# A product of layer one's mixing taken as seven smaller products, with its sums made on chip

## The chip, the cores and the metric

The kernel runs on one core of a Trainium2 chip. The metric is the device time of one execution in microseconds (us), the median of several runs. The engines are called as in the profile: PE is the matrix engine (TensorE), DVE the vector engine, ACT the scalar engine, POOL GpSimd, and SP the engine whose queue issues nearly all the DMAs here.

## The reference

Two layers, each an attention block without softmax and a gated mixer, both added to x (2048 rows of 512):

```python
def _A_ref(x, wqkv, wo):        # 32 heads of 16
    q, k, v = split(x @ wqkv)
    phi = lambda t: where(t > 0, t + 1, exp(t)) + 1e-6
    kv = einsum("bhsd,bhse->bhde", phi(k), v)
    z  = einsum("bhsd->bhd", phi(k))
    o  = einsum("bhqd,bhde->bhqe", phi(q), kv) / (einsum("bhqd,bhd->bhq", phi(q), z) + 1e-6)
    return o @ wo

def _B_ref(x, w_in, w_sp, b_sp, w_out):
    z = gelu(x @ w_in)                       # 512 -> 1792
    z1, z2 = z[..., :896], layernorm(z[..., 896:])
    g = einsum("ts,bsf->btf", w_sp, z2) + b_sp      # w_sp is 2048 x 2048
    return (z1 * g) @ w_out

x = A_x
for _ in range(2):
    x = x + _A_ref(layernorm(x), A_wqkv, A_wo)
    x = x + _B_ref(layernorm(x), B_w_in, B_w_sp, B_b_sp, B_w_out)
```

The change is about the sum over `w_sp`, the mixing.

## The kernel before, in words

**Precision.** Each float32 operand is split into a high part (by ACT) and a low part, the rest (by DVE's `low`, L173, sometimes by POOL, L178). A product is then three matmuls, high by high, high by low and low by high (L184 to L186 for most stages, L1520 to L1522 in the mixing's products).

**Stages of a layer.** The first stage, `P1`, walks over 16 tiles of 128 rows in a loop `s` = 1 to 17: it normalises, makes keys and queries (K, Q; phi at L471, L474, L486; the sum of keys at L492 on POOL) and accumulates the sums G in four banks. `transition` takes G out (L670), sums the keys (zb), multiplies G by the weights of v, masks the blocks (L696) and multiplies by the weights of the output (L706). The second stage, `P2`, is a loop `s` = 1 to 18: it finishes attention (den at L755 to L757, division at L764, product `c`), adds x (`c2`, L798), takes statistics (L315, L317 on DVE; L319 to L322 on POOL), normalises (L328 on ACT), and makes z2 and, in `f`, z1. The transposes and the splits of the next tiles stand between. The third stage, `P4`, is the mixing and the product with `w_out` (`out7`).

**The mixing.** `w_sp` and z2 are seen as 2 x 2 blocks, and the block product is made with seven products instead of eight; their order is `ORDER = ("P2", "P1", "P6", "P7", "P4", "P5", "P3")`. Four of these (P6, P7, P5, P3) multiply sums of blocks of `w_sp`. `Sums` makes these sums in layer one and stores them in DRAM (`s1` to `s4`, float32) for both layers: a `tick` stores the two sums of the last tick, loads up to three pages of `w_sp` ahead, and makes two sums with POOL (L1260). There are 32 ticks for 64 sums of 256 KB. In layer one, eight ticks are in `P1` (steps 2 to 9, in tiles borrowed from the big buffers), fourteen in `P2` (steps 5 to 18) and ten in the first ten steps of the mixing, that is in P2 and in the first steps of P1 (of the mixing).

**Divided products.** A product named in `DIVIDED[layer]` is itself made by the same scheme, as seven smaller ones. An ordinary product has 8 steps `k` of 24 matmuls (8 column groups of 128x512 by three); a divided one has 14 steps of 12 (4 groups by three), two steps for each of the seven, in the order `SEVEN = (1, 5, 6, 2, 7, 3, 4)`. After each pair `evac_div` takes the banks out and combines them. The sums of z2's quarters are made by `zsum` and `zpart` on chip; four sums of quarters of `w_sp`, the tensors `hP` in DRAM (8 pieces of 512 KB for each product), are made before by `halve`: a copy from DRAM to DRAM (SP's queue), then a DMA that adds to what is there (POOL's queue, L1250), each tied `behind` the split of a step's weights. `PARTS` says at which step which of the 32 DMAs goes out. In before only P4 is divided in layer one, and P2 and P4 in layer two; P4's `hP` is made while P1, P6 and P7 of layer one run, P2's while P4 and P5 of layer one run, for layer two.

**What sets the order.** Nothing is scheduled by a program: each engine runs its instructions as the code writes them. Buffers are taken and given back by hand: 22 pages (128x512, `pg`), 6 quads (`qd`), 4 big ones (`bg`, seven sheets of 128x512 each) and 8 PSUM banks. The queue of SP is in order: a store that waits for its data holds up the loads behind it. In the mixing, `fetch(g)` asks for the weights of step g, `sp(g)` splits them (L1350 on ACT, L1351 on DVE), `mm(g)` issues the matmuls, `evac` takes the banks out. `LEAD` says how many steps ahead `P1` loads, `ln_a`, `ln_b` and turns its tiles.

Of the kernel before, what the change touches and what calls it, by code (L numbers as in the profile page):

```python
# [13 lines left out]
OP = mybir.AluOpType  # L14
# [55 lines left out]
        self.slots.put(*self.tiles)  # L70


DIVIDED = (("P4",), ("P2", "P4"))


WRAW = {("P5", 3): (0, 3), ("P5", 6): (1, 4), ("P3", 1): (2, 5), ("P3", 4): (6,)}
# [2 lines left out]
WLONE = ("P3", 5)  # L79
WZ = (0, 1, 2, 3, 4, 5, 6, 7, 8, 9, 10, 11, 12, 13, 14, 15)  # L80
FIRST = 6
LEAD = 6
FIRSTPAIR = 4
EXTRA = (2, 3, 4, 5, 16, 17)
WSTORE = 9
FS = {6: 1, 12: 1, 17: 1}
PARTS = {("P1", k): k - 2 for k in range(2, 8)} | {("P6", k): 6 + k for k in range(8)}
PARTS |= {("P7", 0): 14, ("P7", 1): 15} | {("P4", 2 * k): 16 + k for k in range(7)}
PARTS |= {("P4", 13): 23} | {("P5", k): 24 + k for k in range(8)}


class Sheets:
# [18 lines left out]
def mixer_kernel(ctx: ExitStack, tc: tile.TileContext, x_in, wqkv, wo_d, win1_d, win2_d, wsp_d, bsp_d, wout_d,  # L111
# [291 lines left out]
    class P1:  # L403
# [185 lines left out]
        def run(self, sums):  # L589
            side = deque([self.win2] * NF)  # L590
            ND = NT - DEFER
            for s in range(1, NT + 2):
                for i in self.ahead(s, LEAD - 1, 3):
                    self.loadx(i)
                for i in self.ahead(s, LEAD + 1, 1):
                    self.turn.load(i)
                if 2 <= s < NT:
                    self.T_high(s)
                if s == 1:
                    if not self.kb:  # L600
# [12 lines left out]
                if s == NT + 1:  # L613
                    self.late()
                if s <= NT:
                    self.xsplit(s - 1)
                    self.K_split(s - 1)
                for i in self.ahead(s, LEAD, 2):
                    self.ln_b(i)
                if s <= ND:  # L620
                    self.Q_phi(s - 1)
                if s >= 2:
                    self.Gmm(s - 2)
                if s == NT + 1:
                    self.late_phi()
                if self.L == 0:
                    if s == 2:
                        sums.slots = Sheets(bigs, 2)
                    if 2 <= s < 10:
                        sums.tick(s < 9)  # L630
                    if s == 10:
                        sums.store()
                        sums.slots.close()
                        sums.slots = pages
                if s == 11:
                    self.wv = quads.get([P, 4, 512])
                    nc.sync.dma_start(self.wv, wqkv[:, 1024:1536].rearrange("(c p) f -> p c f", p=P))
                if s == 14:
                    self.wo = quads.get([P, 4, 512])
                    nc.sync.dma_start(self.wo, wo_d.rearrange("(c p) f -> p c f", p=P))  # L640
                if s in range(3,NT-1):
                    self.turn.pre(s + 1)
                if self.L:
                    if s <= 4:
                        self.win2.load(2)
                    else:
                        self.win2.piece()
                    if s == NT - 1:
                        self.win2.sums()
                    if s == NT:  # L650
                        self.win2.last()
                    continue
                if s > 3 and side:
                    side.popleft().piece()
                if s > 2 and side:
                    side[0].fetch()


    def transition(p1, p2):
# [5 lines left out]
        pages.put(za)  # L665
        p1.late()
        p1.wk.free()
        g = quads.get([P, 4, 512])
        for c in range(4):
            (high if c % 2 == 0 else nc.vector.tensor_copy)(g[:, c, :], p1.G[c])  # L670
            banks.put(p1.G[c])
        zb = banks.get(PAGE)
        nc.tensor.matmul(zb, ones, zh, start=True, stop=False)
        nc.tensor.matmul(zb, ones, zl, start=False, stop=True)
# [47 lines left out]
    class P2:  # L722
# [300 lines left out]
        def run(self, sums):  # L1023
# [2 lines left out]
                return  # L1026
            w1 = self.win1
            for s in range(1, NT + 3):
                self.loadx(s + 1)
                self.qturn.load(s + 1)  # L1030
                if s in self.qturn.by_pe:
                    self.c(s - 1)
                    self.b_high(s)
                    self.c2(s - 1)
                    self.p1.late_phi_b()
                    self.b_low(s)
                    if s >= 2:
                        self.d_high(s - 2)
                        self.d_low(s - 2)
                    self.p1.late()  # L1040
                    self.c3(s - 1)
                    self.a2(s + 2)
                    self.p1.late_phi_a()
                    self.a(s + 3)
                else:
                    if s < NT:
                        self.b_high(s)
                    self.a2_den(s + 2)
                    if s < NT:
# [30 lines left out]
                w1.fetch()  # L1080
                if self.L == 0:
                    if s > 4:
                        sums.tick()
# [129 lines left out]
    class Sums:  # L1213
# [3 lines left out]
        def __init__(self):  # L1217
# [2 lines left out]
            self.ahead = deque(self.todo)  # L1220
            self.raw, self.made, self.done = {}, [], []
            self.slots = pages
            self.parts, self.halves = [], {}
# [4 lines left out]
            self.parts = [(what, p, m, q) for p in ("P4", "P2") for what in ("copy", "add") for m in (1, 3, 2, 4)  # L1228
                          for q in range(2)]

        def fetch(self):
# [5 lines left out]
        def halve(self, n, after):  # L1237
# [7 lines left out]
            if what == "copy":  # L1245
                nc.sync.dma_start(self.halves[p, m, q], src)
            else:
                if m in (2, 4):
                    src = self.halves[p, m // 2, q]
                behind(nc.gpsimd.dma_start(self.halves[p, m, q], src, accum_op=OP.add, max_dma_last_dim=4096), after)  # L1250

        def store(self):

# [30 lines left out]
    class P4:  # L1284
# [559 lines left out]
        def run(self, nxt):  # L1844
# [9 lines left out]
            while p2.f():  # L1854
                self.zahead(min(self.zmade, 3))
                n += 1
                if early and n == 4:
                    self.sp(1)
                    self.fetch(5)
            self.zahead(3)  # L1860
            if p2.win1 is not None:
                p2.win1.free()
            if not early:
                self.sp(1)
                self.fetch(5)
            self.gb = [bigs.get([P, NF, 512]) for _ in range(NCHK)]
            n = len(self.steps)
            for g in range(n):
                p, k = self.steps[g]
                self.fetch(g + 5)  # L1870
                evac_first = (p == "P6" or p == "P1" and nxt is not None) and k == HT - 1
                div_first = p in self.div and k == 13 and p == "P4"
                if not evac_first and not div_first:
                    self.sp(g + 2)
                    self.zahead(g + 4 if p in ("P2", "P1") else g + 4)
                self.mm(g)
                if evac_first:
                    if p == "P1":
                        self.ask(3)
                    self.evac(p)  # L1880
                    self.sp(g + 2)
                self.sums.tick()
                if nxt is not None:
                    self.sums.halve(PARTS.get((p, k), -1), self.mark)
                if g == (0 if early else 3):
                    self.loadb()
                if p in self.div:
                    if k % 2 == 1:
# [53 lines left out]
    for L in range(2):  # L1942
# [1 line left out]
        p2 = P2(p1)  # L1944
        p2.loadx(0)
        p2.loadx(1)
        transition(p1, p2)
        p2.p4 = p4 = P4(p2, sums)
        p2.run(sums)
        nxt = P1(1) if L == 0 else None  # L1950
# [33 lines left out]
```

## Time and profile before

| | |
|---|---|
| median of 3 runs | 1361.56 us (1361.43 to 1362.34) |
| profiled execution, its own time | 1362.83 us |
| its span, first to last instruction | 1360.9 us |
| granted PE clock | 1.000 |
| busy, PE / DVE / ACT / POOL | 1353.7 / 985.5 / 694.7 / 420.0 us |
| DMA moved | 260.63 MB, mean 192 GB/s |

A row of a timeline reads: start, duration, engine, line, operation, output<-inputs by the program's names, sizes, number of instructions put together, and in brackets how long the engine was idle before it and what ended that. A row of the waits reads: engine and line, what it waited for, us in total, number of waits, the longest. Line numbers are those of the kernel before.

In the trace of before, layer one's first stage ends near 127 us, the transition reaches to about 141, and the second stage follows.

### The profile page before, as it was taken

Reading aid. Unit: us, or ns where it says so; the run is one execution under the profiler, and the core shown is the slowest. Engines: PE = TensorE matmul, PEld = TensorE weight load, DVE = VectorE, ACT = ScalarE, POOL = GpSimd, SP = SyncE. Lnnn points to the kernel's source line nnn. Section 1 sums busy time; section 2 is a strip of 40 time slices with the busy share of each in tenths; the row PEclk is TensorE's granted clock in tenths of the full one; section 3 lists DMA queues with packets and bytes.
Section 4 is the critical chain, followed back from the end, with each engine's and each line's share of the span. In section 5 each row is a group of like instructions: output and inputs, shape, how many; then the busy total and the mean of one; then the engine's idle time right before and its main releaser. Section 6 shows DMA issues by size and latency. Waiting matters only on the chain.

```text
span 1360.9 us, 18880 instructions
## 1 busy us (share of the span) xinstructions
PE 1353.7 (99%) x6602; PEld 1153.7 (85%) x6602; DVE 985.5 (72%) x1550; ACT 694.7 (51%) x1152; POOL 420.0 (31%) x573
## 2 busy tenths in 40 slices
PE   9999999999999999999999999999999999999998
PEld 7888888888888888889988888888888888888898
DVE  7674877763574798897867777777538757988885
ACT  5764534333432255354676655556666333734454
POOL 3753355544350400301323333545330021021021
PEclk9999999999999999999999999999999999999999
DMA  5872257877995968973675323678777454455344
GB/s 182 276 248 87 79 190 254 297 257 239 323 322 205 288 215 290 258 217 63 145 158 155 115 71 102 204 242 264 226 232 235 153 171 138 155 178 174 112 76 64
DMA packets 155022, 260.63 MB, mean 192 GB/s; under 512 B 13104, under 2 KB 52272, under 8 KB 154672
## 3 DMA queue, kind: packets, MB, share of 16 engines
q1 hardware_dynamic: 140240, 228.50, 50.7%
q0 software_dynamic: 14688, 30.94, 11.5%
q8 instruction: 51, 0.84, 0.2%
q14 instruction: 43, 0.35, 0.1%
HBM read 187.83 MB, written 88.34 MB: 203 GB/s over the span
## 4 chain that ended last, share of the span: by engine, by line
PE 90%; DVE 3%; DMA 2%; POOL 2%; ACT 2%; issue 1%; SPq 0%; DVEq 0%; POOLq 0%; ACTq 0%
PE bank L1520 13%; PE bank L1521 13%; PE bank L1522 13%; PE bank L186 12%; PE bank L184 12%; PE bank L185 12%; PE bank L1718 3%; PE bank L1719 3%; PE bank L1720 3%; PE bank L876 1%; PE bank L877 1%; PE bank L878 1%; DVE st L315 1%; PE bank L1732 1%; PE bank L1731 1%
## 5 line engine op out<-in xcount | busy, mean ns | idle before, releaser
L1520 PE MATMUL bank<-qd,pg 128*128 128x512 f32 x776 | 301.9, 389 | 0.0
L1521 PE MATMUL bank<-qd,pg 128*128 128x512 f32 x776 | 301.9, 389 | 0.0
L1522 PE MATMUL bank<-qd,pg 128*128 128x512 f32 x776 | 301.9, 389 | 0.0
L1351 DVE TENSOR_TENSOR qd<-qd,qd 128x1024 fp32r<-128x1024 f32 x130 | 162.6, 1253 | 84.9 <-ACT qd L1350 84.7
L1350 ACT ACTIVATE qd<-qd 128x1024 fp32r<-128x1024 f32 x130 | 136.8, 1053 | 151.6 <-PE bank L1522 135.7
L186 PE MATMUL bank<-qd,pg 128*128 128x512 f32 x496 | 193.4, 390 | 0.0
L1522 PEld LDWEIGHTS bank<-qd,pg 128*128 128x128 f32 x776 | 145.7, 188 | 30.4
L1520 PEld LDWEIGHTS bank<-qd,pg 128*128 128x128 f32 x776 | 145.7, 188 | 30.1
L1521 PEld LDWEIGHTS bank<-qd,pg 128*128 128x128 f32 x776 | 145.7, 188 | 30.1
L184 PE MATMUL bank<-qd,pg 128*128 128x512 f32 x356 | 139.0, 390 | 0.6 <-DVE pg L173 0.6
L185 PE MATMUL bank<-qd,pg 128*128 128x512 f32 x356 | 138.7, 390 | 0.0
L1561 POOL TENSOR_TENSOR bg<-bg,pg 128x512 f32<-128x512 f32 x28 | 48.2, 1723 | 243.7 <-DVE bg L1575 124.6
L186 PEld LDWEIGHTS bank<-qd,pg 128*128 128x128 f32 x496 | 93.1, 188 | 19.9 <-DVE pg L173 0.4
L319 POOL TENSOR_SCALAR rs<-mv 128x1 f32<-128x1 f32 x80 | 24.4, 304 | 212.0 <-DVE mv L317 203.5
L328 ACT ACTIVATE pg<-pg,nb,rs 128x512 f32<-128x512 f32 x52 | 42.1, 811 | 88.8 <-POOL nb L322 87.8
L1720 PE MATMUL bank<-wo,qd 128*128 128x256 f32 x288 | 81.5, 283 | 0.0
L184 PEld LDWEIGHTS bank<-qd,pg 128*128 128x128 f32 x356 | 66.8, 188 | 14.9 <-DVE pg L173 1.0
L185 PEld LDWEIGHTS bank<-qd,pg 128*128 128x128 f32 x356 | 66.8, 188 | 13.9 <-DVE qd L173 0.3
L1260 POOL TENSOR_TENSOR pg<-pg,pg 128x512 f32<-128x512 f32 x48 | 67.1, 1398 | 37.3 <-DMA pg<-in_wsp_dram 35.3
L1718 PE MATMUL bank<-wo,qd 128*128 128x256 f32 x276 | 78.1, 283 | 0.0
L1719 PE MATMUL bank<-wo,qd 128*128 128x256 f32 x276 | 78.0, 283 | 0.0
L1390 ACT ACTIVATE pg<-pg 128x384 fp32r<-128x384 f32 (+1 forms) x32 | 18.5, 579 | 100.4 <-DVE pg L1388 55.0
(224 smaller groups left out, 3078.7 us busy)
## 6 DMA issues: line engine op xcount, KB each, us to landing
qd<-s SPq DMA_DIRECT2D x64, 512.0 KB, 3.7
qd<-in_wsp_dram SPq DMA_DIRECT2D x42, 512.0 KB, 4.5
pg<-z SPq DMA_DIRECT2D x56, 256.0 KB, 3.9
pg<-w POOLq DMA_DIRECT2D x56, 256.0 KB, 5.5
pg<-in_wsp_dram SPq DMA_DIRECT2D x48, 256.0 KB, 4.5
z<-pg SPq DMA_DIRECT2D x48, 256.0 KB, 3.3
s<-pg SPq DMA_DIRECT2D x48, 256.0 KB, 4.2
qd<-hP SPq DMA_DIRECT2D x24, 512.0 KB, 3.9
```

The lines of the kernel that those rows point to most:

```text
L184: nc.tensor.matmul(out, ah, bh, start=start, stop=False)
L185: nc.tensor.matmul(out, ah, bl, start=False, stop=False)
L186: nc.tensor.matmul(out, al, bh, start=False, stop=stop)
L1260: nc.gpsimd.tensor_tensor(t, a, b, op=OP.add)
L1350: self.mark = nc.scalar.activation(w[:, 0], r, AF.Copy)
L1351: nc.vector.tensor_sub(w[:, 1], r, w[:, 0].bitcast(F32))
L1520: m(out, h[:, o], w[:, 0, j, :], start=start, stop=False, skip_group_check=True)
L1521: m(out, h[:, o], w[:, 1, j, :], start=False, stop=False, skip_group_check=True)
L1522: m(out, l[:, o], w[:, 0, j, :], start=False, stop=stop, skip_group_check=True)
L1718: m(out, A, x, start=start and f == 0, stop=False, skip_group_check=True)
L1719: m(out, A, y, start=False, stop=False, skip_group_check=True)
L1720: m(out, B, x, start=False, stop=stop and f == 2, skip_group_check=True)
```

## The change

Layer one's product P2 is divided too. For that its `hP` must exist before the mixing of layer one, so it is made in the first half, by loads, adds and stores:

- `load2` loads four pages of `w_sp` (in steps 9, 10 and 11 of `P1` into sheets of the big buffers, in step 14 into pages); `add2` makes four sums of each group, 16 in all, of 128x512, on DVE (12: one in steps 12 and 13, two in steps 14, 15 and 16, four in the transition behind the copies of G) or on POOL (4: one in steps 13 and 14, two in step 15); `store2` stores them, one SP store of 256 KB each. P2's 8 copies and 8 adding DMAs go from `PARTS`; layer two reads the same `hP`. P4's DMAs go out two steps later, and none is left in P4 or P5.
- The ticks move: still eight in `P1`; one behind the transition, one in each of steps 1 to 4 of `P2` as well as in steps 5 to 18, one more at the head of step 18; the last four (`LEFT`) in steps g = 15 to 18 of the mixing, where layer one's P1 now stands, and their last stores in g = 19. The sums of the last tick in `P2` are stored in the loop of the last z1 products. A new first fetch stands in the transition.
- `LEAD` is 8 where it was 6, in both layers: the lookahead of `P1` grows two steps later.
- In layer one, the weights of the mixing's second step are made inside the loop of the last z1 products (`SPN`), the b_sp load comes at g = 0 instead of 3, and P1's banks are taken out behind `sp(g + 2)` instead of ahead of it.

```diff
-DIVIDED = (("P4",), ("P2", "P4"))
+DIVIDED = ("P2", "P4"), ("P2", "P4")
...
-LEAD = 6
+LEAD = 8
...
-PARTS = {("P1", k): k - 2 for k in range(2, 8)} | {("P6", k): 6 + k for k in range(8)}
-PARTS |= {("P7", 0): 14, ("P7", 1): 15} | {("P4", 2 * k): 16 + k for k in range(7)}
-PARTS |= {("P4", 13): 23} | {("P5", k): 24 + k for k in range(8)}
+PARTS = {("P1", 4 + k): k for k in range(4)} | {("P6", k): 4 + k for k in range(8)}
+PARTS |= {("P7", k): 12 + k for k in range(4)}
+LEFT = 4
+SPN = 3
+LOAD2 = (9, 10, 11, 14)
+DVE2 = {12: 1, 13: 1, 14: 2, 15: 2, 16: 2}
+POOL2 = {13: 1, 14: 1, 15: 2}
...
                     if s == 10:
                         sums.store()
-                        sums.slots.close()
-                        sums.slots = pages
+                    sums.store2()
+                    if s in LOAD2:
+                        sums.load2(pages if s > 12 else sums.slots)
...
+                if self.L == 0:
+                    sums.add2(1, POOL2.get(s, 0))
+                    sums.add2(0, DVE2.get(s, 0))
...
         p1.wk.free()
+        if p1.L == 0:
+            sums.store2()
+            sums.slots.close()
+            sums.slots = pages
+            sums.fetch()
...
+        if p1.L == 0:
+            sums.add2(0, 4)
         zb = banks.get(PAGE)
...
             for s in range(1, NT + 3):
+                if s == NT + 2:
+                    sums.tick()
...
                     self.a(s + 3)
+                    sums.tick()
...
+        def load2(self, slots):
+
+            k = self.groups.popleft()
+            a, b, c, d = (load(wsp_d[2 + j, HT + k + s], slots) for s, j in ((0, 0), (0, 1), (4, 0), (4, 1)))
+            self.adds[k == 2].extend([(1, k, d, b, d, ()), (3, k, b, a, b, ()), (2, k, a, a, d, (slots, b, d)), (4, k, c, c, a, (slots, a, c))])
+
+        def add2(self, pool, n):
+            for _ in range(n):
+                m, k, o, a, b, done = self.adds[pool].popleft()
+                (nc.gpsimd if pool else nc.vector).tensor_tensor(o, a, b, op=OP.add)
+                self.made2.append((m, k, o, done))
+
+        def store2(self):
+
+            for m, k, t, done in self.made2:
+                nc.sync.dma_start(self.halves["P2", m, k // 2][k % 2], t)
+                if done:
+                    done[0].put(*done[1:])
+            self.made2 = []
...
-                if early and n == 4:
+                if not early and n == 1:
+                    self.sums.store()
+                if n == (4 if early else SPN):
                     self.sp(1)
                     self.fetch(5)
...
-                evac_first = (p == "P6" or p == "P1" and nxt is not None) and k == HT - 1
+                evac_first = p == "P6" and k == HT - 1
...
-                self.sums.tick()
+                if not early and g == 14:
+                    self.sums.fetch()
+                if not early and 15 <= g <= 15 + LEFT:
+                    self.sums.tick()
...
-        transition(p1, p2)
+        transition(p1, p2, sums)
+        if L == 0:
+
+            sums.store2()
+            sums.tick()
```

How the engines' instructions moved, at three places. The order of DVE, from the end of layer one's first stage into the transition, before (L474 and L486 are phi, L670 the copy of G out of the banks, L685 the first instruction behind the transition's sum of keys):

```order
L474 SCALAR_TENSOR_TENSOR pg_161_1404<-bank_47_1391,pg_161_1404 128x512
L173 TENSOR_TENSOR pg_163_1409<-pg_141_1239,pg_162_1408 128x512
L486 SCALAR_TENSOR_TENSOR pg_165_1413<-pg_161_1404,pg_164_1412 128x512
L474 SCALAR_TENSOR_TENSOR z_q_1454<-bank_48_1429,z_q_1454 128x512
L663 TENSOR_SCALAR pg_20_307<-pg_20_307 128x512
L670 COPY qd_7_1480<-bank_10_397 128x512
L670 COPY qd_7_1480<-bank_12_399 128x512
L474 SCALAR_TENSOR_TENSOR z_q_1492<-bank_49_1467,z_q_1492 128x512
L685 TENSOR_REDUCE zeps<-pg_170_1488 128x32
```

and in the changed kernel (lines are its own, higher by 4 to 15; L1280 is `add2`):

```order
L490 SCALAR_TENSOR_TENSOR pg_169_1449<-pg_165_1440,pg_168_1448 128x512
L1280 TENSOR_TENSOR bg_1_412<-bg_1_412,bg_2_413 128x512
L1280 TENSOR_TENSOR bg_2_413<-bg_2_413,bg_1_412 128x512
L478 SCALAR_TENSOR_TENSOR z_q_1496<-bank_48_1471,z_q_1496 128x512
L671 TENSOR_SCALAR pg_20_307<-pg_20_307 128x512
L683 COPY qd_7_1530<-bank_10_397 128x512
L683 COPY qd_7_1530<-bank_12_399 128x512
L1280 TENSOR_TENSOR pg_158_1369<-pg_156_1365,pg_158_1369 128x512
L1280 TENSOR_TENSOR pg_156_1365<-pg_155_1363,pg_156_1365 128x512
L1280 TENSOR_TENSOR pg_155_1363<-pg_155_1363,pg_158_1369 128x512
L1280 TENSOR_TENSOR pg_157_1367<-pg_157_1367,pg_155_1363 128x512
L478 SCALAR_TENSOR_TENSOR z_q_1546<-bank_49_1511,z_q_1546 128x512
```

Two adds now stand behind step 16's phi, and four between the copies of G and the phi of a late query tile (L478), all with two inputs in pages or sheets.

The order of POOL at the start of layer one's second stage, before (L743 multiplies queries by the sum of keys for den, L178 makes a low part, L319 to L322 finish the statistics):

```order
L743 TENSOR_TENSOR pg_181_1603<-z_q_569,pg_170_1488 128x512
L319 TENSOR_SCALAR rs<-mv 128x1
L320 TENSOR_TENSOR rs<-rs,mhalf 128x1
L322 TENSOR_SCALAR nb<-mv,rs 128x1
L743 TENSOR_TENSOR pg_188_1676<-z_q_660,pg_170_1488 128x512
L178 TENSOR_TENSOR bg_6_1679<-pg_172_1496,bg_5_1678 128x512
```

and in the changed kernel (L1299 are the adds of a tick):

```order
L758 TENSOR_TENSOR pg_188_1657<-z_q_569,pg_177_1542 128x512
L1299 TENSOR_TENSOR pg_175_1526<-pg_174_1524,pg_175_1526 128x512
L1299 TENSOR_TENSOR pg_174_1524<-pg_174_1524,pg_176_1528 128x512
L323 TENSOR_SCALAR rs<-mv 128x1
L324 TENSOR_TENSOR rs<-rs,mhalf 128x1
L326 TENSOR_SCALAR nb<-mv,rs 128x1
L758 TENSOR_TENSOR pg_196_1738<-z_q_658,pg_177_1542 128x512
L1299 TENSOR_TENSOR pg_176_1528<-pg_175_1526,pg_176_1528 128x512
L1299 TENSOR_TENSOR pg_190_1673<-pg_176_1528,pg_190_1673 128x512
L182 TENSOR_TENSOR bg_6_1751<-pg_179_1550,bg_5_1750 128x512
```

The first tick stands ahead of the first tile's statistics, the second between L758 and the low part of a weight (L182).

The order of SP's queue about the transition, before (L640 loads wo, the rest of it the first x tiles and weights of the second stage):

```order
L640 DMA qd_6_1345<-in_wo_dram 128x4x512
L154 DMA pg_166_1458<-in_x_dram 128x512
L154 DMA pg_167_1460<-in_x_dram 128x512
L154 DMA pg_172_1496<-in_win_dram 128x512
L154 DMA pg_173_1498<-in_win_dram 128x512
```

and in the changed kernel, from the last four of the nine stores of `hP` (L1286) that now stand between wo and x:

```order
L1286 DMA hP_1_0_141<-bg_2_413 128x512
L1286 DMA hP_3_0_143<-bg_2_413 128x512
L1286 DMA hP_2_0_142<-bg_1_412 128x512
L1286 DMA hP_4_0_144<-bg_2_413 128x512
L158 DMA pg_170_1502<-in_x_dram 128x512
L158 DMA pg_171_1504<-in_x_dram 128x512
L158 DMA pg_174_1524<-in_wsp_dram 128x512
L158 DMA pg_175_1526<-in_wsp_dram 128x512
L158 DMA pg_176_1528<-in_wsp_dram 128x512
L158 DMA pg_179_1550<-in_win_dram 128x512
```

The loads of x, of the first tick and of the weights wait behind these stores, and these for the adds.

More of the change, by code (lines that the diff above doesn't have):

```diff
@@ L656, in run, with transition @@
                     side[0].fetch()
-    def transition(p1, p2):
+    def transition(p1, p2, sums):
         wv, wo = p1.wv, p1.wo
@@ L1082, in run @@
                     if s > 4:
-                        sums.tick()
+                        sums.tick(s < NT + 2)
                     if s >= WSTORE and s < WSTORE + NF:
@@ L1222, in __init__ @@
             self.slots = pages
+            self.groups, self.adds, self.made2 = deque(range(4)), (deque(), deque()), []
             self.parts, self.halves = [], {}
@@ L1227, in __init__ @@
                         self.halves[p, m, q] = dram.tile([2, P, 512], F32, name=f"h{p}_{m}_{q}")
-            self.parts = [(what, p, m, q) for p in ("P4", "P2") for what in ("copy", "add") for m in (1, 3, 2, 4)
+            self.parts = [(what, p, m, q) for p in ("P4",) for what in ("copy", "add") for m in (1, 3, 2, 4)
                           for q in range(2)]
@@ L1863, in run @@
             if not early:
-                self.sp(1)
-                self.fetch(5)
+                assert len(self.sums.todo) == LEFT
             self.gb = [bigs.get([P, NF, 512]) for _ in range(NCHK)]
@@ L1877, in run @@
                 if evac_first:
[L1878 to L1879 removed]
                     self.evac(p)
                     self.sp(g + 2)
[L1882 removed]
+                if not early and g == 14:
+                    self.sums.fetch()
+                if not early and 15 <= g <= 15 + LEFT:
+                    self.sums.tick()
                 if nxt is not None:
                     self.sums.halve(PARTS.get((p, k), -1), self.mark)
[L1885 removed]
+                if g == 0:
                     self.loadb()
```

## The prediction

> **What bounds the kernel now.** I read the page first, then the list of waits, the table of windows, and the timelines of the stretches that the change touches.
>
> ```profile
> span 1360.9 us, 18880 instructions
> PE 1353.7 (99%) x6602; PEld 1153.7 (85%) x6602; DVE 985.5 (72%) x1550; ACT 694.7 (51%) x1152; POOL 420.0 (31%) x573
> PE 90%; DVE 3%; DMA 2%; POOL 2%; ACT 2%; issue 1%; SPq 0%; DVEq 0%; POOLq 0%; ACTq 0%
> ```
>
> TensorE is busy for all but 7.2 of 1360.9 us, and the chain of waits that ended last is 90% PE. The waits of PE, all of them:
>
> ```profile
> PE bank L567 <- DVE pg L562: 2.3, 1, 2.3
> PE bank L184 <- DVE pg L173: 0.6, 1, 0.6
> PE bank L184 <- ACT qd L170: 0.3, 1, 0.3
> ```
>
> The first lies at the kernel's start, the second in layer one's first stage; the third comes back below. So the time is the number of matmuls times their pace: a matmul taken out is paid in full, unless a wait that is now hidden comes out. For the pace I took windows of 40 us; the columns are the stretch, its length, then busy us and instructions of PE, weight loads, DVE, ACT and POOL, the granted clock, the DMA share and GB/s:
>
> ```profile
> 120.00:160.00 40.00, 40.00 (x199) 32.53 (x198) 28.20 (x53) 19.95 (x35) 13.59 (x15) 1.00 0.22 73
> 160.00:200.00 40.00, 39.68 (x191) 34.33 (x190) 29.37 (x50) 19.16 (x32) 20.51 (x31) 1.00 0.49 158
> 200.00:240.00 40.00, 39.86 (x184) 34.02 (x183) 31.19 (x47) 16.10 (x27) 23.80 (x33) 1.00 0.79 263
> 320.00:360.00 40.00, 40.00 (x183) 34.01 (x182) 12.44 (x18) 18.50 (x27) 14.03 (x17) 1.00 0.71 244
> 360.00:400.00 40.00, 40.00 (x178) 33.15 (x177) 29.75 (x30) 11.07 (x14) 23.58 (x16) 1.00 1.02 356
> 1040.00:1080.00 40.00, 40.00 (x179) 33.10 (x178) 35.71 (x54) 19.37 (x27) 0.00 (x0) 1.00 0.59 184
> ```
>
> Where the mixing's products run (360 to 400 in layer one, 1040 to 1080 in layer two) a window holds 178 to 179 matmuls of 128x512 at clock 1.00, so one takes 40/178 = 0.2247 us. The page's group of the same matmuls has a larger number:
>
> ```profile
> L1520 PE MATMUL bank<-qd,pg 128*128 128x512 f32 x776 | 301.9, 389 | 0.0
> ```
>
> Its 389 ns is the duration of one that overlaps its neighbours (301.9/776 = 0.389); it is no price of a matmul taken away.
>
> **The change, part by part.** *The seven.* Layer one's product P2 now runs as 14 steps of 12 matmuls, 168, where it was 8 steps of 24, 192. That removes 24 x 0.2247 = **5.4 us** of PE time. The Trainium skill has a lower price in "TensorE: Matmul & The Clock Gate", section "Back-to-back issue gap": it calls N/2.4 + 2.5 ns an isolated gap and gives some 131 ns a matmul at N = 512 for a sustained stream, by which I estimate 24 x 0.131 = 3.1 us and a time of about 1359.1 with the same waits. The windows of this kernel, sustained streams with weight loads, disagree (224.7 ns), and the trace decides.
>
> What pays for it on the other engines is an additional combination at each pair of steps, which layer two already does: its divided P2 is the 1040 window, where DVE is at 35.7 of 40 us and PE waits for nothing. In layer one's 320 window DVE has 12.4 of 40, so it can take the same work. There is one difference: layer one enters the product from the last z1 products, with the second step's weights now made inside that loop, behind its third z1 product. I take 0, with 0 to 0.5 us as the range.
>
> *Making the quarter sums on chip.* 16 loads, 16 adds and 16 stores of 256 KB go into steps 9 to 16 of layer one's first stage and the transition. In return, eight copies and eight accumulating DMAs leave the products P4 and P5; nothing on PE waited there, so I count no gain. 12 adds go to DVE. Its timeline at the end of the first stage:
>
> ```profile
> 105.05 0.69 DVE L474 SCALAR_TENSOR_TENSOR pg<-bank,pg 128x512 f32<-128x512 f32 x1 [1.36 <-ACT pg L471]
> 121.22 0.69 DVE L474 SCALAR_TENSOR_TENSOR pg<-bank,pg 128x512 f32<-128x512 f32 x1 [3.30 <-ACT pg L471]
> 122.61 0.69 DVE L486 SCALAR_TENSOR_TENSOR pg<-pg,pg 128x512 fp32r<-128x512 f32 x1
> 126.66 0.69 DVE L474 SCALAR_TENSOR_TENSOR z_q<-bank,z_q 128x512 f32<-128x512 f32 x1 [3.36 <-ACT z_q L471]
> 127.59 1.28 DVE L670 COPY qd<-bank 128x512 f32<-128x512 f32 x2
> 133.06 0.69 DVE L474 SCALAR_TENSOR_TENSOR z_q<-bank,z_q 128x512 f32<-128x512 f32 x1 [4.18 <-PE bank L695]
> 136.06 0.82 DVE L696 TENSOR_TENSOR pg<-bank,mask 128x128 f32<-128x128 f32 x4
> ```
>
> Two adds a step (steps 14 to 16) are 2 x 0.69 = 1.38 us into gaps of 3.3 us; the four of the transition, 2.76 us, stand between the copies (ending at 128.87) and the L474 at 133.06, in a gap of 4.18 us. If the price stays 0.69, all of it is hidden. It doesn't stay so beside a POOL add:
>
> ```profile
> 30.15 2.99 POOL L1260 TENSOR_TENSOR bg<-bg 128x512 f32<-128x512 f32 x2 [3.66 <-DMA bg<-in_wsp_dram]
> 30.24 1.75 DVE L173 TENSOR_TENSOR pg<-pg,pg 128x512 fp32r<-128x512 f32 x1
> 31.91 1.77 DVE L486 SCALAR_TENSOR_TENSOR pg<-pg,pg 128x512 fp32r<-128x512 f32 x1
> ```
>
> DVE operations with two pages as inputs took 1.75 and 1.77 there against 0.69: 1.1 us more each. POOL's work near these places, with the four new POOL adds to come into steps 13 to 15:
>
> ```profile
> 118.06 1.29 POOL L492 TENSOR_TENSOR pg<-pg,pg 128x512 f32<-128x512 f32 x1 [4.21 <-DVE pg L486]
> 123.44 1.29 POOL L492 TENSOR_TENSOR pg<-pg,pg 128x512 f32<-128x512 f32 x1 [4.09 <-DVE pg L486]
> 128.43 1.30 POOL L178 TENSOR_TENSOR pg<-pg,pg 128x512 fp32r<-128x512 f32 x1 [3.70 <-ACT pg L170]
> 131.95 5.02 POOL L743 TENSOR_TENSOR pg<-z_q,pg 128x512 f32<-128x512 f32 x4 [2.23 <-ACT pg L677]
> ```
>
> In a step (5.4 us, 118.06 to 123.44) POOL's L492 starts just behind L486, where DVE's new adds start too: one of two is hit, 1.38 + 1.1 = 2.5 us against 3.3. Only step 15, with two POOL adds more (2.6 us), can hit both adds and one of the next operations: 1.38 + 3 x 1.1 = 4.7, which is 1.4 us over. L486's output is needed a step later, so I take 0.2 us of PE wait here, between 0 and 1.4. In the transition the L178 at 128.43 and the four L743 from 131.95 frame the adds: two or three of four are hit, 2.76 + 2.2 to 3.3 = 5.0 to 6.1 us against 4.18, or 0.8 to 1.9 late. Behind them stands the chain L474, L685 to L757, L696, for which PE waits next:
>
> ```profile
> 137.41 1.88 PE L706 MATMUL bank<-qd,pg 128*128 128x512 f32 x4
> ```
>
> L696 ends at 136.88, 0.53 us ahead of it. So 0.3 to 1.4 us of wait; if POOL is the one held up instead, 0. I take 0.4.
>
> *The ticks.* A tick (two POOL adds, two stores, up to three loads) came with steps 5 to 18 of the second stage and ten times in P2 and P1. Now one comes ahead of the stage, one in each of steps 1 to 4, one more in step 18, and four in P1. POOL's gaps there and the tick that before had first:
>
> ```profile
> 154.76 1.29 POOL L178 TENSOR_TENSOR bg<-pg,bg 128x512 fp32r<-128x512 f32 x1 [3.57 <-ACT bg L170]
> 161.66 1.30 POOL L178 TENSOR_TENSOR bg<-pg,bg 128x512 fp32r<-128x512 f32 x1 [2.96 <-ACT bg L170]
> 176.23 0.23 POOL L319 TENSOR_SCALAR rs<-mv 128x1 f32<-128x1 f32 x1 [2.57 <-DVE mv L317]
> 192.18 2.69 POOL L1260 TENSOR_TENSOR pg<-pg,pg 128x512 f32<-128x512 f32 x2 [2.93 <-DMA pg<-in_wsp_dram]
> 196.24 0.81 ACT L328 ACTIVATE pg<-pg,nb,rs 128x512 f32<-128x512 f32 x1 [7.96 <-POOL nb L322]
> 197.63 0.47 PE L184 MATMUL bank<-bg,qd 128*128 128x448 f32 x1 [0.27 <-ACT qd L170]
> ```
>
> A tick of 2.69 us fits gaps of 2.57 to 3.57. The first one waited 2.93 us for its loads, its statistics (L319 to L322) stood behind it, ACT's L328 behind those, and PE waited 0.27 us: the third wait of the list. So there a tick may be late by 2.93 - 0.27 = 2.7 us before PE feels it. With loads a tick ahead this wait goes: 0.3 gained. The new ticks run beside DVE operations, of which one per tick, 1.1 us longer, lies ahead of work that PE waits for; the 200 window shows ticks in every step, with DVE at 31.2 of 40 and PE at 39.86. I take 0.3 for all, 0 to 1.1. In P1, four ticks take the place of the ten that stood in P2 and P1, where PE stood still nowhere: 0.
>
> *The rest.* On SP's queue the first two x loads and the second stage's first weights now stand behind nine stores that wait for adds, the last of them of step 16, before the copies at 127.59. The first x is used here:
>
> ```profile
> 146.96 0.69 DVE L798 TENSOR_TENSOR pg<-pg,bank 128x512 f32<-128x512 f32 x1 [0.47 <-PE bank L186]
> ```
>
> That is 19 us later, so nothing is lost. The first stage's column loads are asked for two steps earlier (LEAD), which moves no matmul. P1's results are taken out behind the next weights' making instead of ahead: layer two does so already. 0 for all three, with 0.5 as the upper end for what I overlook.
>
> **The sum.** -5.4 + 0.2 + 0.4 + 0.3 - 0.3 = -4.8 us. The profiled execution took 1362.83 us (span 1360.9); it would take 1358.0. Its runs' median is 1361.56, so I forecast **1356.8 us**. With all bounds at their best, -5.4 - 0.3 = -5.7, or 1355.9; with waits of 1.4 in the first stage, 1.4 in the transition and 1.1 in the ticks, -5.4 + 3.9 - 0.3 = -1.8, or 1359.8.
>
> **Rivals.** *Lock.* Every collision of DVE and POOL counts: the upper ends just named hold, and the time is 1358.0 to 1359.8. For it: the 1.75 us rows. Against: before's ticks in fourteen steps met the same DVE operations, and PE waited 0.3 us in all. The Trainium skill states it as a rule in "SBUF — State Buffer", section "Who interferes with whom": a DVE instruction with two SBUF inputs contends with a GpSimd instruction that reads SBUF, the shared ports are an exclusive lock, and issue order decides who blocks. The rows agree on the size, and show DVE as the one held up. Chance 0.19.
>
> *Ticks wait for loads* (the slower side). The ticks' loads stand on SP behind stores that wait for adds on DVE and POOL. The page of waits has such loads late in before:
>
> ```profile
> POOL pg L1260 <- DMA pg<-in_wsp_dram: 35.3, 10, 14.4
> pg<-in_wsp_dram SPq DMA_DIRECT2D x48, 256.0 KB, 4.5
> ```
>
> Ten waits, 3.5 us on average. If all five early ticks wait 3.5 us, and the room is not 2.7 but halfway to the 0.53 us of the transition, 1.6, PE waits 5 x 1.9 = 9.5 us: 1361.56 - 5.4 + 9.5 = 1365.7. It is slower than before from 1.6 + 5.4/5 = 2.7 us of wait per tick. Against: a load lands in 4.5 us, is asked for a tick ahead (7 us, from 154.76 to 161.66), and DMA is at 0.22 in the 120 window. Chance 0.07.
>
> *The division is paid for by DVE.* If layer one's P2 came to be bound by DVE, at 35.7 of 40 us plus POOL collisions from the tick left at its entry, the gain would shrink by at most a step or so (2.7 us): 1359.5. Layer two's window speaks against it. Chance 0.06. *The gain is 389 ns each:* 9.3 us, 1352.9; the windows exclude it nearly: 0.02.
>
> **Chances and range.** Forecast 0.66, lock 0.19, late ticks 0.07, DVE 0.06, larger gain 0.02. A measurement of this kernel can tell about 0.2%, 2.7 us, from no change, so faster means under 1358.8: the forecast, the larger gain and somewhat over half of the lock: 0.78. Within: the rest of the lock and DVE, 0.15. Slower: the late ticks, 0.07. The range goes from 1355.6 (the best sum, less 0.3 for the spread of a median) to 1359.8, which leaves out the late ticks, the larger gain and a little of the others.
>
> **What would show it.** After: 6578 PE instructions, and no wait of PE over 1 us but the one at L567. Right if the windows of layer one's P2 hold 178 or 179 matmuls with DVE near 36 of 40 and POOL near 0. The lock shows as DVE operations of 1.4 to 1.8 us in the first stage's steps 14 to 16 and in the transition, with a PE wait for the L696 product or its like. Late ticks show as POOL waits for in_wsp_dram between 145 and 180 us, and PE waits behind ACT there. The forecast is wrong if PE's waits grow by more than 2.5 us, or if its span shrinks with no fewer matmuls.

## The result and the profile after

The changed kernel took 1355.86 us (median of 6 runs, 1355.2 to 1357.71) against 1361.49 (6 runs): 5.6 us less, a ratio of 0.9959 with a 95% interval of 0.9947 to 0.9972. The forecast was 1356.8 in a range of 1355.6 to 1359.8. The head of its page, to be held against that of before:

```profile
span 1354.1 us, 18993 instructions
PE 1347.2 (99%) x6578; PEld 1147.9 (85%) x6578; DVE 1015.1 (75%) x1602; ACT 704.7 (52%) x1172; POOL 426.5 (31%) x569
```

PE has 24 instructions fewer and is 6.5 us less busy; DVE has 30 us more to do. All waits of PE in the changed kernel:

```profile
PE bank L571 <- DVE pg L566: 2.3, 1, 2.3
PE bank L188 <- DVE pg L177: 0.3, 1, 0.3
PE bank L188 <- ACT pg L174: 0.2, 1, 0.2
```

The wait of 2.3 us is that of the start, the 0.3 is the first stage's (0.6 before), and before's 0.3 of the old first tick is gone. The 0.2 is new and lies at the start, at 7.5 us; none came in the transition or beside the ticks of layer one. The windows that answer to those of before (the last, in layer two, starts 5 us earlier for the shift):

```profile
120.00:160.00 40.00, 40.00 (x200) 32.53 (x199) 35.92 (x60) 19.38 (x34) 24.19 (x22) 1.00 0.67 227
160.00:200.00 40.00, 40.00 (x195) 35.28 (x194) 30.77 (x54) 19.61 (x33) 29.54 (x41) 1.00 0.70 218
360.00:400.00 40.00, 40.00 (x178) 33.13 (x177) 38.93 (x56) 20.01 (x28) 5.79 (x4) 1.00 0.72 223
1035.00:1075.00 40.00, 40.00 (x178) 33.12 (x177) 36.94 (x56) 19.02 (x26) 0.00 (x0) 1.00 0.57 184
```

The third row holds most of layer one's divided P2, which runs from 351.2 to 389.2 us: the pace is the old one, 178 matmuls in 40 us, and DVE stands at 38.9 of 40. POOL's 5.8 us belong to the first two of the four late ticks, which start at 394.0, behind the product.

The window starts 8.8 us into the product. As far into layer two's P2, which was divided already, DVE is just as busy (the first row is of the changed kernel, the second of before):

```profile
1025.70:1065.70 40.00, 40.00 (x177) 32.86 (x176) 38.94 (x60) 21.44 (x31) 0.00 (x0) 1.00 0.68 219
1032.80:1072.80 40.00, 40.00 (x178) 33.10 (x178) 39.75 (x62) 20.84 (x30) 0.00 (x0) 1.00 0.69 218
```

PE waits for nothing in either.

Matching the two traces matmul by matmul shows where the 6.8 us of span between these two executions lie. At the 24 removed matmuls the changed kernel's lead grows from 1.6 to 7.0 us: 5.4 us. The lead of 1.6 us ahead of that is made of 0.7 us at the start, ahead of anything that the change touches, of gains near 48 us (0.3), 198 us (0.9, at the old first tick) and 235 us (0.3), and of a loss near 285 us (0.6). Between 53 and 195 us, where the new loads, the 16 adds, the transition and the ticks of steps 1 to 4 lie, the lead stands still, at 0.96 to 0.98 us: there the added work costs PE nothing. The start, the first 24 us, holds 88 matmuls in before and 91 here:

```profile
4.62 2.33 PE L567 MATMUL bank<-pg,ones 128*128 128x512 f32 x5
```

```profile
4.62 1.56 PE L571 MATMUL bank<-pg,ones 128*128 128x512 f32 x5
```

The first row is before, the second after: the same five matmuls took 2.33 and 1.56 us, as the first matmuls start 0.43 us apart until 6.8 us in before and only until 5.0 here. Other executions of the changed kernel and its edits show either, or values between. So the 0.7 us are scatter, and the median's 5.6 us is the better measure of the change.

### The profile page after: what moved, and what is told of

Its sections match the earlier page's. It is cut to its first block, busy times and chain, and to the rows that moved or that the text cites. A ratio compares the mean times of both kernels' runs of the same rounds, so it can differ in the third digit from the quotient of the medians.

```text
span 1354.1 us, 18993 instructions
## 1 busy us (share of the span) xinstructions
PE 1347.2 (99%) x6578; PEld 1147.9 (85%) x6578; DVE 1015.1 (75%) x1602; ACT 704.7 (52%) x1172; POOL 426.5 (31%) x569
## 4 chain that ended last, share of the span: by engine, by line
PE 80%; DMA 1%; DVE 1%; POOL 1%; ACT 0%; SPq 0%; issue 0%; DVEq 0%; POOLq 0%
PE bank L1560 13%; PE bank L1561 13%; PE bank L1559 13%; PE bank L190 9%; PE bank L188 9%; PE bank L189 9%; PE bank L1757 3%; PE bank L1758 3%; PE bank L1759 3%; PE bank L892 1%; PE bank L891 1%; PE bank L893 1%; PE bank L1771 1%; PE bank L1770 1%; PE bank L1772 1%; DMA yt<-pg 0%
## 5 line engine op out<-in xcount | busy, mean ns | idle before, releaser
L1390 DVE TENSOR_TENSOR qd<-qd,qd 128x1024 fp32r<-128x1024 f32 x136 | 171.3, 1262 | 66.4 <-ACT qd L1389 66.2
L1389 ACT ACTIVATE qd<-qd 128x1024 fp32r<-128x1024 f32 x136 | 143.1, 1053 | 132.1 <-PE bank L1561 115.1
L1600 POOL TENSOR_TENSOR bg<-bg,pg 128x512 f32<-128x512 f32 x28 | 51.4, 1835 | 302.2 <-ACT qd L1389 175.5
L1299 POOL TENSOR_TENSOR pg<-pg,pg 128x512 f32<-128x512 f32 x48 | 66.7, 1390 | 58.8 <-DMA pg<-in_wsp_dram 56.7
L174 ACT ACTIVATE pg<-pg 128x512 fp32r<-128x512 f32 x77 | 48.0, 624 | 58.1 <-DVE pg L402 21.5
```

The costliest lines, as they stand in the source:

```text
L1299: nc.gpsimd.tensor_tensor(t, a, b, op=OP.add)
L1389: self.mark = nc.scalar.activation(w[:, 0], r, AF.Copy)
L1390: nc.vector.tensor_sub(w[:, 1], r, w[:, 0].bitcast(F32))
```

## The experiments

All are edits of the changed kernel. Times are medians; the kernel before took 1361.5 to 1361.7 beside them.

**What a matmul is worth.** Layer two's P2 is taken whole again:

```diff
-DIVIDED = ("P2", "P4"), ("P2", "P4")
+DIVIDED = ("P2", "P4"), ("P4",)
...
-            for p in DIVIDED[1]:
+            for p in DIVIDED[0]:
```

(The second edit keeps the tensors of the quarter sums, which layer one needs.)

> The changed kernel, with layer two's product P2 taken whole again: 24 matmuls of 128x512 more and nothing else moved ahead of it. By the pace of the windows (224.7 ns a matmul) it is 5.4 us slower than the changed kernel's 1355.9, so 1361.3, within 0.5. If a matmul cost its 389 ns it would be 9.3 us more, 1365.2; at 131 ns, 3.1 us more, 1359.0. PE has no wait in layer two in either kernel, so nothing else should come out.

Measured: 1360.95 us (1360.02 to 1364.67), 5.1 more than the changed kernel. Its page has 6602 PE instructions again, and in the window of layer two's P2 DVE has much less to do (21.6 us against 36.9) at the same pace of PE:

```profile
1035.00:1075.00 40.00, 40.00 (x179) 33.11 (x178) 21.64 (x30) 11.80 (x16) 0.00 (x0) 1.00 0.27 92
```

Matmul by matmul, the 24 cost 5.4 us. A matmul's price is the time from its start to the next one's, 0.227 us in these products (40 us over the 178 of a window, which counts parts of matmuls at both ends, gives 0.225); the readings of 389 and 131 ns are out.

**The sums without the seven.** Layer one's P2 is whole, all else kept; the last ticks stay in the same steps of P1, whose number is now lower:

```diff
-DIVIDED = ("P2", "P4"), ("P2", "P4")
+DIVIDED = ("P4",), ("P2", "P4")
...
-                if not early and g == 14:
+                if not early and g == 8:
-                if not early and 15 <= g <= 15 + LEFT:
+                if not early and 9 <= g <= 9 + LEFT:
```

> The changed kernel, with layer one's product P2 taken whole again (8 steps of 24 matmuls), but the quarter sums made on chip in the first half as in the change, and the ticks where the change has them; the last four ticks stand in the same steps of P1. Theory: the sums and the ticks are hidden, and all of the gain is the 24 matmuls: 1355.9 + 5.4 = 1361.3, level with before within 0.5. Rival, that the sums cost 1 us or more and the seven saves more than 5.4: 1362 or above. Rival, that the moved ticks themselves bring a part of the gain: 1360.5 or below.

Measured: 1361.55 us, against before a ratio of 1.0002 (0.9993 to 1.0011). So the 16 loads, adds and stores, the moved ticks and the other small moves together cost nothing that can be told and bring nothing, within some 1.5 us by that interval; the gain is the 24 matmuls.

**The lookahead.** `LEAD` is 6 again.

> The changed kernel with LEAD 6 in place of 8. Theory: the first stage's early step has its PE wait of 0.6 us back where the change shows 0.3, so 1356.1 within 0.3, which is too little to tell from none in the times; in the profile the wait at L188 behind DVE L177 near 48 us is 0.6. Rival: the longer lookahead gives the bandwidth to the new loads, and without it steps 9 to 14 wait: 1357 or more.

Measured: 1355.25 us (1354.75 to 1356.67), not slower, and the wait of 0.6 us near 48 us, which was expected back, isn't in its page, whose only wait of PE is the 2.3 us of the start. So that wait doesn't come from the shorter lookahead alone. The changed kernel run again beside another kernel took 1355.89 (1355.13 to 1356.63).

> The changed kernel itself, once more, as the measure for the next one on the same chip: 1355.9 within 0.6.

> The changed kernel with LEAD 6 and with all 16 quarter sums on DVE, the two edits that cost nothing alone. If LEAD 6 is worth something, 1355.3 or below, and below the changed kernel run beside it by 0.5 or more; if the 0.6 us that it seemed to gain is the scatter of small waits, level with it within 0.5.

The second of these, with `LEAD` 6 and all sums on DVE, took 1356.07 (1355.77 to 1357.81). So the 0.6 us of `LEAD` 6 is not a gain that holds; the longer lookahead is not needed in this kernel, nor does it hurt. No version here beats the changed kernel by more than the spread of its runs.

**All sums on one engine.** First on DVE, then on POOL:

```diff
-DVE2 = {12: 1, 13: 1, 14: 2, 15: 2, 16: 2}
-POOL2 = {13: 1, 14: 1, 15: 2}
+DVE2 = {12: 1, 13: 2, 14: 3, 15: 4, 16: 2}
+POOL2 = {}
...
-            self.adds[k == 2].extend([...])
+            self.adds[0].extend([...])
```

> The changed kernel, with all 16 quarter sums on DVE (1, 2, 3, 4 and 2 in steps 12 to 16, four in the transition) and none on POOL. Four DVE adds more are 2.8 us, four POOL adds fewer take away up to four collisions of 1.1 us. Theory: even, no wait, 1355.9 within 0.6. Rival, that DVE's steps 14 and 15 overrun (3.4 + 2.8 = 6.2 us of 5.4) by more than their cover: 1357 or more.

```diff
+DVE2 = {}
+POOL2 = {12: 2, 13: 2, 14: 2, 15: 3, 16: 3}
...
-            sums.add2(0, 4)
+            sums.add2(1, 4)
...
-            self.adds[k == 2].extend([...])
+            self.adds[1].extend([...])
```

> The changed kernel, with all 16 quarter sums on POOL (2, 2, 2, 3 and 3 in steps 12 to 16, four in the transition) and none on DVE. Three POOL adds and L496 are 5.2 us of a step of 5.4, and each holds up a DVE operation with two page inputs by up to 1.1 us; in the transition four adds, 5.2 us, stand ahead of L758, whose result DVE needs ahead of the masks L711. Lock as the rival had it: DVE and POOL late by 2 to 3 us, PE waits 1.5 to 3 us in the transition, 1357.5 to 1361. If collisions fall where DVE has room: 1355.9 within 0.6.

Measured: 1356.26 us on DVE (1354.46 to 1356.45), level with the changed kernel; 1357.79 on POOL (1357.18 to 1358.99), 1.9 more. On POOL nearly all of the loss is one wait, in the transition. POOL, DVE and PE there:

```profile
129.74 5.34 POOL L1280 TENSOR_TENSOR pg<-pg,pg 128x512 f32<-128x512 f32 x4
135.04 2.52 POOL L758 TENSOR_TENSOR pg<-z_q,pg 128x512 f32<-128x512 f32 x2
```

```profile
136.36 0.69 DVE L770 TENSOR_REDUCE den<-pg 128x32 f32<-128x512 f32 x1 [2.62 <-POOL pg L758]
137.91 0.82 DVE L711 TENSOR_TENSOR pg<-bank,mask 128x128 f32<-128x128 f32 x4
```

```profile
138.20 1.12 PE L721 MATMUL bank<-qd,pg 128*128 128x512 f32 x2 [1.53 <-DVE pg L711]
```

Four adds ahead of L758 make den late; L711 stands behind den on DVE, though it doesn't need it, and PE waits 1.53 us for L711. It is queue order rather than the lock: the four adds took 5.34 us, 1.33 each, against 1.29 for one that nothing disturbs.

**How much cover DVE has.** Each of DVE's twelve adds is made twice, first into a spare page:

```diff
+                if not pool:
+                    t = pages.get(PAGE)
+                    nc.vector.tensor_tensor(t, a, b, op=OP.add)
+                    pages.put(t)
                 (nc.gpsimd if pool else nc.vector).tensor_tensor(o, a, b, op=OP.add)
```

> The changed kernel, with each of DVE's twelve quarter sums made twice, first into a spare page (12 more DVE adds of 128x512, two inputs each: two to four more in a step, four more in the transition). It asks how much cover is left. In the changed kernel the transition's four adds took 3.65 us and left 0.61 us idle behind them; four more, with one more collision, take 3.9 to 5 us: the L478 behind them is 3.3 to 4.4 us late, and PE's next product has 0.5 to 1 us of room. Theory, that the cover is nearly used up: PE waits 2 to 4 us and loses some more while its clock comes back, 1358.5 to 1362. Rival, that a wide cover hid the adds: 1355.9 within 0.6.

Measured: 1365.14 us (1362.31 to 1367.52), 9.3 more than the changed kernel and 0.2% slower than before (1.0011 to 1.0029). It is more than was expected, since the adds of steps 14 to 16 make PE wait too (from 118 us on). PE's waits in the profiled execution, without that of the start and one of 0.2:

```profile
PE bank L721 <- DVE pg L711: 2.3, 1, 2.3
PE bank L190 <- DVE pg L177: 1.8, 1, 1.8
PE bank L188 <- ACT pg L489: 1.0, 1, 1.0
PE bank L689 <- POOL pg L182: 0.8, 1, 0.8
```

Four waits of 5.9 us in places where the changed kernel has none. With the slower matmuls behind them they cost 9.4 us by the matched traces (this kernel is 0.2 us behind the changed one from 48 to 116 us, and 9.6 at 149). PE is slowest after the longest: four L721 took 3.25 us here and 1.88 in the changed kernel, where nothing held them up (second row).

```profile
144.21 3.25 PE L721 MATMUL bank<-qd,pg 128*128 128x512 f32 x4 [2.28 <-DVE pg L711]
136.43 1.88 PE L721 MATMUL bank<-qd,pg 128*128 128x512 f32 x4
```

So twelve adds, 8.3 us of DVE work at 0.69 each, are hidden, and twelve more cost more than their own 8.3 us.

**Ticks beside the divided product.** The last four ticks stand in steps 5 to 8, inside the divided P2:

```diff
-                if not early and g == 14:
+                if not early and g == 4:
-                if not early and 15 <= g <= 15 + LEFT:
+                if not early and 5 <= g <= 5 + LEFT:
```

> The changed kernel with the last four ticks (eight POOL adds) in steps 5 to 8 of the mixing, beside the divided P2, where DVE is at 38.9 of 40 us, in place of steps 15 to 18, beside P1. Rival of the division paid by DVE: DVE has 1.1 us in 40 free, each POOL add holds it up by 0.5 to 1.1 us, 4 to 8.8 us in all, and the nearest cover of PE there is 2.2 us: PE waits 2 to 6 us, 1358 to 1362. Theory that DVE is still far enough from being the bound: no wait, 1355.9 within 0.5.

Measured: 1361.29 us (1359.48 to 1363.87); the whole gain is gone. POOL and DVE in the stretch:

```profile
368.75 8.83 POOL L1299 TENSOR_TENSOR pg<-pg,pg 128x512 f32<-128x512 f32 x4 [26.08 <-DMA pg<-in_wsp_dram]
379.18 4.90 POOL L1299 TENSOR_TENSOR pg<-pg,pg 128x512 f32<-128x512 f32 x3 [1.60 <-DMA pg<-in_wsp_dram]
```

```profile
377.15 1.04 DVE L1480 SCALAR_TENSOR_TENSOR pg<-z_z,pg 128x256 fp32r<-128x256 f32 x2 [3.46 <-DMA s<-pg]
379.32 2.21 DVE L1390 TENSOR_TENSOR qd<-qd,qd 128x1024 fp32r<-128x1024 f32 x1
381.45 2.91 DVE L1460 TENSOR_TENSOR pg<-z_z,pg 128x256 f32<-128x256 f32 x2
```

```profile
381.58 0.65 PE L1560 MATMUL bank<-qd,pg 128*128 128x512 f32 x1 [2.04 <-DVE qd L1390]
382.02 0.63 PE L1561 MATMUL bank<-qd,pg 128*128 128x512 f32 x1
...
384.58 0.63 PE L1561 MATMUL bank<-qd,pg 128*128 128x512 f32 x1
...
390.17 0.50 PE L1560 MATMUL bank<-qd,pg 128*128 128x512 f32 x1 [1.00 <-DVE qd L1390]
```

Two things make DVE late. It waits 3.46 us for a page that still holds a tick's sum until its store (`s<-pg`) has landed, and then, beside POOL's adds, a split takes 2.21 us (1.22 without POOL) and two sums take 2.91 (0.75 in the changed kernel). PE waits 2.04 us, its next eight matmuls start 0.43 us apart instead of 0.23, a further 1.6 us, and it waits another 1.00 us at 390. By the matched traces the stretch costs 5.5 us in all, which is the loss. Of DVE's two delays the lock was expected and the page was not. POOL was held up too (the four adds of its first row took 8.83 us against 4 x 1.29 = 5.2), so its stores came later; how much of PE's wait each delay makes was not measured apart.

**Late ticks.** The ticks ahead of step 5 don't ask for their pages a tick ahead:

```diff
-                    sums.tick()
+                    sums.tick(False)
```

(in step s = 1 to 4, and the same behind the transition.)

> The changed kernel, with the ticks ahead of the second stage and in its steps 1 to 4 not loading a tick ahead: those of steps 2 and 4 ask for their pages when they are due and wait some 4.7 us for them on POOL, with the statistics behind them. It prices the rival of the late ticks. With the 2.7 us of room that the old first tick showed: PE waits 2 x 2.0 = 4 us, 1360; with the 1.6 that the rival assumed, 2 x 3.1, 1362; if PE has more room there than that: 1356 to 1358.

Measured: 1360.79 us (1358.29 to 1361.45), 4.9 more than the changed kernel. The profiled execution, 1358.53, is one of two of eleven near 1358.4; the other nine took 1360.2 to 1361.5. In it one tick, not two, waited for its loads:

```profile
179.06 3.19 POOL L1299 TENSOR_TENSOR pg<-pg,pg 128x512 f32<-128x512 f32 x2 [4.74 <-DMA pg<-in_wsp_dram]
192.43 2.99 POOL L1299 TENSOR_TENSOR pg<-pg,pg 128x512 f32<-128x512 f32 x2
```

```profile
197.52 0.81 ACT L332 ACTIVATE pg<-pg,nb,rs 128x512 f32<-128x512 f32 x1 [5.94 <-POOL nb L326]
```

```profile
198.91 0.47 PE L188 MATMUL bank<-bg,qd 128*128 128x448 f32 x1 [2.02 <-ACT qd L174]
```

The tick at 179 waited 4.74 us for its pages. PE still had enough work there, and paid 2.02 us 20 us later, behind the next tick's statistics, at the same product as before's 0.27. The difference, 4.74 - 2.02 = 2.7 us, is the value read from before's trace (2.93 - 0.27), but in part by luck. In before the tick that waited stands directly ahead of these statistics; here it is the tick before that, and POOL makes up 1.9 us in between: in the changed kernel the two ticks start at 173.88 and 189.16, so the first is 5.2 us late here and the second 3.3. Counted at the second, the room is only 3.3 - 2.0 = 1.3 us.

One late tick makes 1355.9 + 2.0 = 1357.9, near the two at 1358.4. What the other nine lost beside that stays open, as no profile caught one. That PE's clock dropped behind the wait, as in the two kernels above, would fit the size, and the mean granted clocks point that way: 1.000 in the two, 0.998 or 0.999 in each of the nine, as in the profiled executions of the two kernels above (0.999). The changed kernel has 0.999 in single executions too (at 1356.81 us), so this is a hint; no trace shows it.

## Why the prediction was right

The direction, the cause and the main term hold; the three costs put beside the main term were not there. Point by point:

- **24 matmuls at 0.2247 us, 5.4 us.** Held: 5.4 us in the matched traces, 5.1 by the median with layer two's P2 whole, 5.7 with layer one's. The Trainium skill's 131 ns a matmul ("TensorE: Matmul & The Clock Gate", "Back-to-back issue gap") gives 3.1 us, and neither run that puts the 24 back agrees with it.
- **Division costs nothing on other engines: 0, range 0 to 0.5.** Held, though both windows behind it were read wrongly. Layer two's divided P2 runs from 1024.0 to 1061.9 us in before, so the 1040 window (35.7 of 40) holds only 22 us of it; the window from 1032.8 has DVE at 39.75, and still PE doesn't wait. Layer one's 320 window (12.4 of 40) lies mostly ahead of its P2, which ran from 352.7 to 396.2 us in before, with DVE busy for 31.5 of these 43.5 us. Divided it has 34.1 of 38.0. So there was less to spare than was thought, and "near 36 of 40" was no sign to go by. The rival that DVE pays (0.06) is wrong for the change as it is; with POOL's ticks beside the product, PE does wait for DVE.
- **Quarter sums in steps 12 to 16: 0.2; transition: 0.4.** The mis-sized terms, with the ticks' 0.3: together 0.9 us, measured none (the lead that stands still from 53 to 195 us). The collisions were there, as the changed kernel's DVE rows show:

```profile
118.34 1.67 DVE L1280 TENSOR_TENSOR bg<-bg,bg 128x512 f32<-128x512 f32 x1
...
121.63 1.77 DVE L490 SCALAR_TENSOR_TENSOR pg<-pg,pg 128x512 fp32r<-128x512 f32 x1
123.32 2.38 DVE L1280 TENSOR_TENSOR bg<-bg,bg 128x512 f32<-128x512 f32 x2
...
127.81 3.65 DVE L1280 TENSOR_TENSOR pg<-pg,pg 128x512 f32<-128x512 f32 x4
132.07 0.69 DVE L478 SCALAR_TENSOR_TENSOR z_q<-bank,z_q 128x512 f32<-128x512 f32 x1 [0.61 <-PE bank L710]
```

  The price of some 1.1 us each held roughly: these rows have 0.9 to 1.1. In the transition the count was too high: I took two or three of the four adds as hit, and one was (3.65 us for the four instead of 4 x 0.69 = 2.76), because POOL is idle between L182 (to 128.73) and L758 (from 130.97):

```profile
112.82 1.74 POOL L1280 TENSOR_TENSOR bg<-bg 128x512 f32<-128x512 f32 x1
...
127.44 1.29 POOL L182 TENSOR_TENSOR pg<-pg,pg 128x512 fp32r<-128x512 f32 x1 [2.29 <-ACT pg L174]
130.97 2.86 POOL L758 TENSOR_TENSOR pg<-z_q,pg 128x512 f32<-128x512 f32 x2 [2.23 <-ACT pg L692]
```

  They ended 0.61 us ahead of the L478 behind them. In steps 14 to 16 DVE's idle time went from over 3 us a step to almost none, without PE feeling it.
- **0.3 gained at the old first tick.** Held: that wait is gone. In this pair of traces it brought 0.9, as the matmuls behind the wait start more slowly in before.
- **The ticks of steps 1 to 4 fit POOL's gaps.** Held: POOL's idle time of 2.6 to 3.6 us per step went to 1.3 or none, and PE waited 0.0 there, between 120 and 200 us. Late ticks did not come, since their loads had landed. The price of a late one, 2.0 us of PE wait, came out as read in the late-tick run, but with a room that is made up otherwise than was thought.
- **The lock as a rival (0.19)** fails by its cost to PE, not by its kind: the longer DVE operations came, and no PE wait behind them. The Trainium skill's rule ("SBUF — State Buffer", "Who interferes with whom") holds in these rows, and the loser can be either: POOL's add of 1.29 us took 1.74 beside one of DVE's (112.82, above; 1.66 for DVE's at 113.45).
- **What would show it.** 6578 instructions and no new wait over 1 us: as written. DVE "near 36 of 40" was not. The median came out 0.9 below the forecast, the size of the three terms that were not there; as single executions lie between 1355.2 and 1357.7, the match to a tenth is luck.

## What to carry to other kernels

Where PE is busy 99% of the span, price a matmul taken out by the count in a window, not by its mean duration, and spend the work on cover that the trace shows to be idle. Cover has an edge: twelve adds of 0.69 us were free here and twelve more cost 9.3 us, so place added work by the gaps of each step. A window's busy share depends on where the window starts: here windows of the same kind of product showed DVE at 35.7 to 39.75 of 40 us, so cut windows by the product's own start and end. A wait read from before's trace (one tick waiting 2.9 us, PE waiting 0.3) gives the room for that tick and that product; for a tick one further ahead the sum is another, since the engine makes up a part of the delay in between.

## What the runs showed of the hardware

A pause of PE can cost more than its length. Behind the wait of 2.04 us in the run with ticks beside the divided product, eight matmuls started 0.43 us apart, and the granted clock there fell. It fell in the same way behind the wait of 2.28 us in the run with the adds made twice (second row):

```profile
382.00:386.00 4.00, 4.00 (x12) 2.99 (x10) 4.00 (x4) 1.56 (x2) 2.60 (x3) 0.60 1.05 401
144.00:148.00 4.00, 3.79 (x8) 1.90 (x9) 3.17 (x10) 1.62 (x3) 1.26 (x1) 0.60 0.02 4
```

The column behind POOL's is the granted clock, 0.60 in these 4 us. The 2.02 us of the late tick's run had no such effect in the profiled execution: the granted clock stayed at 1.00, and the next matmuls started at their usual distance within 1 us. Nor had the waits of 1.53 us (all sums on POOL) and 1.83 us (adds made twice), behind which it stayed at 1.00 too. The Trainium skill ("TensorE: Matmul & The Clock Gate", "What's actually happening") puts the fall of the clock behind at least one idle window of some 3.4 us; here waits of 2.0 to 2.3 us were followed by it in two cases of three.
